# A fused attention and MLP kernel: the first batch's token softmax and state reads are placed later in the written order, and two pairs of loads change places

## The chip, the cores and the metric

The kernel runs on one core of one Trainium2 chip. The metric is the device time of a run in microseconds (us); before is the median of 3 runs. Besides the runs there is one profiled execution, whose span and time are given below.

## What is computed

```
x (8, 8, 512, 64), state (8, 8, 32, 64), float32          # batch, head, rows, 64 columns
scores  = x @ state^T / 8;   a  = softmax(scores)          # 512 x 32 per head
xread   = a @ state                                        # 512 x 64
scores2 = state @ x^T / 8;   a2 = softmax(scores2)         # 32 x 512 per head
sread   = a2 @ x                                           # 32 x 64
X = [xread; sread], heads side by side -> (8 * 544, 512)
h = X @ w_in (512 x 2048);  g = max(h, 0) + alpha * min(h, 0)
out = g @ w_out (2048 x 512), float32                      # (4352, 512)
```

For the 512 token rows of a batch the kernel never forms xread: it multiplies the states into w_in first (`m` = state @ w_in, per batch 256 x 2048) and then the softmax weights by `m`. The 32 state rows of each batch (sread) are collected and go through w_in and w_out together as a ninth "batch".

## The kernel before

Everything is done in the order of a string, `ORDER` (lines 17 to 102), which is read token by token at the end of the function. A token is a step with its arguments; each engine gets its instructions in that order and waits by semaphores. Nothing is reordered. `a`, `v` and `p` in a token name the engine that does a copy or a shift: ScalarE (ACT), VectorE (DVE), GpSimd (POOL). In `F.0.8.4` batch 0, slice 8 of 16, PSUM bank 4 are meant.

The steps, b being the batch:

- Loads, all issued by POOL's queue: `lx0` (x of batch 0 in two halves, L178), `lst` (states, L191), `wi.f` (w_in, four blocks of 512 columns, L197), `wo.i` (w_out, four blocks of 512 rows, L203), `lx.b` (x, L162).
- x transposed: for batches 0 and 1 on PE (`xt`, L277, copied out by `xo`, L282); for the others by a DMA transpose from SP's queue (`xd`, L269) into a rotating buffer `xT`.
- `Z` (L216): matmuls of zeros that fill PE at the start. `stt`, `str` transpose the states; `sto`, `sro` copy them out.
- `sc.b` (L291): both score products in one, into the PSUM tile `two` (two banks). `sc.0.0` and `sc.0.1` are batch 0's halves; `sc.0` computes them again as a whole.
- State softmax (over 32 states, for the token rows): `sb` transpose (L324, L326), `smax` (L332), `ssh` shift (L338), `sexp` (L344), `ssum` (L348, L349), `snorm` (L352), `wb` transpose back (L360) into `aT`, the weights. Batch 0 goes through it in halves.
- Token softmax (over 512 tokens, for the state rows): `tm` maximum (L372, L375), `te.b.g` exponential (L383) from `two`, `tsum` reciprocal (L393), `tn` norm on POOL (L397), `tt` DMA transpose from SP's queue (L401), `rd` the reads a2 @ x on PE (L416), `rdo` copy out (L427). Its buffers `e2` have two places, and a place is free when `tt` has landed.
- `m.b.f` (L441): 8 matmuls in 64 x 32 tiles, in `two` or in two single banks; `mo` copies them to `m`, one bank at a time (L463).
- First product: `F` (L474, two matmuls), or `f` for one half of it (L495). `N` on ACT (L506) and `G` on DVE (L514) make g of it and set the bank free.
- Second product: `S.b.q.j` (L526, two matmuls; eight of them make a 128 x 512 output), `O` copies it out (L564) and SP's queue writes it (L567). `R`, `L`, `RO`, `LO` do the same for the state rows and the last output in pieces.

There are six single banks and `two`. Each new use of a bank waits for the copy or the `G` that empties it. `xg` (x as loaded) has 4 places in SBUF, `xT` 2, `m` 7.

Of the kernel before, what the change touches and what calls it, by code (L numbers as in the profile page):

```python
# [46 lines left out]
S.1.3.5 N.2.8 S.1.3.6 G.2.7 F.2.6.2 O.1.0.a N.2.6 m.3.3.1.0 G.2.8 sc.4 rd.1.5 snorm.p.3 F.2.5.3
G.2.6 mo.3.3.a.0 F.2.14.1 rdo.1.a wb.3 N.2.5 tsum.3 S.2.1.0.2 F.2.11.5 mo.3.3.a.1 G.2.5 S.1.3.7
N.2.14 F.2.10.0 F.3.4.3 G.2.14 N.2.11 S.2.1.1 F.3.1.1 lx.5 O.1.3.v N.3.4 S.2.1.2 N.2.10 G.2.11 tt.2
S.2.0.0.4 S.2.1.3 S.2.0.1 G.2.10 F.3.14.5 F.3.9.0 S.2.1.4 tn.3.1 N.3.1 N.3.9 G.3.1 S.2.1.5 S.2.0.2  # L50
G.3.4 tn.3.0 N.3.14 tm.4 F.3.3.1 F.3.8.3 G.3.14 N.3.8 G.3.9 S.2.1.6 S.2.1.7 S.2.0.3 S.2.3.0.5 N.3.3
xd.5 O.2.1.a tt.3 sb.4 G.3.8 smax.4 F.3.6.0 F.3.2.2 te.4.0 S.2.3.1 S.2.3.2 N.3.6 N.3.2 F.3.13.3
S.2.0.4 te.4.1 ssh.p.4 N.3.13 G.3.3 G.3.6 S.2.0.5 F.3.7.1 G.3.2 S.2.0.6 N.3.7 S.2.0.7 sexp.4 G.3.13
G.3.7 S.2.3.3 S.2.3.4 S.2.3.5 m.6.0 O.2.0.v m.5.1.0.2 mo.6.0.a.1 mo.5.1.a.1 rd.3.3 mo.6.0.v.0
rdo.3.a mo.5.1.v.0 rd.2.1 m.4.1.4.2 ssum.4 sc.5 m.4.3.0.3 rdo.2.a S.2.3.6 mo.4.1.a.1 mo.4.1.a.0 tm.5
tsum.4 snorm.p.4 F.3.5.1 mo.4.3.a.0 mo.4.3.a.1 F.3.0.2 F.3.10.4 N.3.0 S.2.3.7 O.2.3.a S.2.2.0.0
S.2.2.1 F.3.11.3 G.3.0 wb.4 S.2.2.2 S.3.3.0.5 F.3.15.2 S.3.3.1 N.3.5 lx.6 G.3.5 te.5.0 te.5.1 N.3.10
N.3.15 S.2.2.3 F.3.12.1 S.2.2.4 N.3.11 S.3.3.2 lx.7 N.3.12 G.3.10 G.3.15 F.4.6.4 N.4.6 tn.4.0
# [577 lines left out]
```

## Time and profile before

| | us |
|---|---|
| median of 3 runs (218.6 to 219.0) | 218.71 |
| profiled execution, its own time | 219.66 |
| its span | 217.9 |
| PE busy | 210.6 |
| first `f` on PE (L495) | 16.23 |
| first `S` on PE (L526) | 20.89 |
| ACT copies of the states (L259), two | 9.56 to 11.64 |

The span is the time from the first to the last instruction on the chip; what lies around it (1.76 us) is not seen in the trace. A line of the timeline has the start, the length, the engine, the line of the kernel, the operation, what it writes and reads, how many, and in brackets the idle time before it and who ended it. Matmuls overlap, so a pair that starts every 0.43 us is shown as 0.59 us long. PEld is PE's weight load. A line of the windows has, for each stretch, the busy time of PE, PEld, DVE, ACT and POOL with the number of instructions, then the granted PE clock, the busy share of the DMA engines and what they moved. DMA issues take time on the queue's engine; the time to landing is counted from the issue.

Time to landing of the first loads, from the views of their tiles: w_in block 0, issued at 4.05, took 7.6 us; x of batch 1, issued at 4.80, 9.5; w_in 1 at 5.68, 11.6; w_out 0 at 12.45, 7.3; w_in 2 at 15.75, 7.2; w_out 1 at 16.55, 8.5; w_in 3 at 17.29, 10.3; w_out 2 at 23.53, 7.4; x of batch 2 at 25.90, 7.7; w_out 3 at 29.98, 8.9; x of batch 3 at 41.34, 9.0. The DMA transposes of x took 7.7 (issued at 33.71), 5.3 (50.48), 3.7, 3.7, 4.8 and 3.7 us; those of the token weights 3.5, 6.9 (47.21), 3.9, 3.1, 3.3, 3.1 and 4.2.

### The profile page before, as it was taken

The page shows a single profiled execution, that of the slowest core. Times are in us where ns is not written, and L with a number is a line of the kernel's source. Part 1 is how long each engine was busy: PE and PEld are TensorE (multiplying, and loading weights), DVE is VectorE, ACT ScalarE, POOL GpSimd, SP SyncE. Part 2 cuts the span into 40 slices and gives each one's busy share as a digit, 9 for nine tenths or more (in the row PEclk, how much of TensorE's full clock was granted, in tenths as well). Part 3 has the DMA queues.
Part 4 walks back from the last instruction along what each step waited for, and adds up shares of the span by engine and source line. Part 5 has one row for each costly group of instructions (what it writes and reads, how often), then busy time and mean ns, then how long its engine had stood idle before and what let it go on. Part 6 is the DMA issues. An engine that isn't in the chain of part 4 may idle for free.

```text
span 217.9 us, 4311 instructions
## 1 busy us (share of the span) xinstructions
PE 210.6 (97%) x1698; PEld 104.2 (48%) x1698; DVE 165.2 (76%) x250; ACT 137.4 (63%) x271; POOL 71.0 (33%) x58
## 2 busy tenths in 40 slices
...
GB/s 69 188 199 206 200 171 117 206 196 113 92 143 100 92 245 101 51 88 187 249 55 99 96 48 53 0 99 48 50 148 3 46 48 51 48 33 15 51 96 144
DMA packets 41748, 23.12 MB, mean 106 GB/s; under 512 B 24192, under 2 KB 38016, under 8 KB 41728
## 3 DMA queue, kind: packets, MB, share of 16 engines
q0 software_dynamic: 12704, 8.62, 28.5%
...
q14 instruction: 7, 0.06, 0.1%
...
## 4 chain that ended last, share of the span: by engine, by line
PE 84%; DMA 9%; DVE 3%; POOL 1%; issue 1%; ACT 0%; POOLq 0%
PE o L526 47%; PE h L474 23%; DMA xT<-xg 4%; DMA w_in_sb<-in_moe_w_in_dram 3%; PE m_ps L441 3%; PE h L483 3%; PE o L574 3%; DMA xg<-in_x_dram 2%; PE o L546 2%; PE sr_ps L416 2%; PE sc L291 1%; POOL an L352 1%; DVE ts L326 1%; DVE m L463 1%; DVE mx L332 1%
## 5 line engine op out<-in xcount | busy, mean ns | idle before, releaser
L526 PE MATMUL o<-w_out_sb,gt 128*128 128x512 f16 x496 | 125.3, 379 | 0.9 <-DMA w_out_sb<-in_moe_w_out_dram 0.9
L506 ACT ACTIVATE neg<-h 128x512 f32<-128x512 f32 (+1 forms) x144 | 77.1, 579 | 47.8 <-PE h L474 38.4
L514 DVE SCALAR_TENSOR_TENSOR gt<-neg,oma_sb,h 128x512 f16<-128x512 f32 x128 | 89.9, 738 | 16.5 <-ACT neg L506 15.6
L526 PEld LDWEIGHTS <-gt 128*128 128x128 f16 x496 | 47.3, 98 | 56.4 <-issue 4.5
L474 PE MATMUL h<-aT,m 128*128 128x512 f16 x250 | 68.3, 379 | 0.0
L474 PEld LDWEIGHTS <-m 128*128 128x128 f16 x250 | 24.1, 98 | 28.4 <-issue 0.6
L397 POOL TENSOR_SCALAR e<-e,r 128x512 f16<-128x512 f16 x16 | 25.0, 1566 | 20.4 <-DVE r L393 16.6
L463 ACT CAST m<-m_ps 128x512 f16<-128x512 f32 x50 | 27.1, 606 | 4.6 <-PE m_ps L441 4.3
L352 POOL TENSOR_TENSOR an<-ts,r 128x1024 f16<-128x1024 f32 (+1 forms) x9 | 15.4, 1719 | 33.2 <-DVE r L349 14.8
L338 POOL TENSOR_TENSOR ts<-ts,mx 128x1024 f32<-128x1024 f32 (+1 forms) x9 | 15.5, 1720 | 30.9 <-DVE mx L332 30.9
L564 ACT COPY osb<-o 128x512 f32<-128x512 f32 x22 | 12.9, 591 | 14.9 <-PE o L526 14.9
L441 PE MATMUL m_ps<-w_in_sb,stT 64*32 64x512 f16 x256 | 11.3, 383 | 0.6 <-DMA w_in_sb<-in_moe_w_in_dram 0.4
L383 ACT ACTIVATE e<-sc,nb 128x512 f16<-128x512 f32 x16 | 11.1, 700 | 1.1 <-DVE nb L375 1.1
L360 DVE STREAM_TRANSPOSE aT<-an 128x1024 f16<-128x1024 f16 (+1 forms) x9 | 10.1, 1120 | 1.9 <-POOL an L352 1.9
L514 DVE SCALAR_TENSOR_TENSOR gs<-neg,oma_sb,h 128x256 f16<-128x256 f32 x16 | 7.5, 476 | 4.5 <-ACT neg L506 4.5
L463 DVE CAST m<-m_ps 128x512 f16<-128x512 f32 x14 | 9.1, 679 | 2.0 <-ACT m L463 1.6
L372 DVE TENSOR_REDUCE nb<-sc 128x2 f32<-128x1024 f32 x8 | 9.6, 1202 | 0.5 <-PE sc L291 0.5
L332 DVE TENSOR_REDUCE mx<-ts 128x32 f32<-128x1024 f32 (+1 forms) x9 | 9.8, 1091 | 0.0
L348 DVE TENSOR_REDUCE r<-ts 128x32 f32<-128x1024 f32 (+1 forms) x9 | 9.8, 1087 | 0.0
L483 PE MATMUL h<-XS,w_in_sb 128*128 128x256 f16 x64 | 9.4, 273 | 0.0
L584 DVE COPY osr<-o 128x512 f32<-128x512 f32 x1 | 0.7, 692 | 11.3 <-PE o L574 11.3
L344 ACT ACTIVATE ts<-ts 128x1024 f32<-128x1024 f32 (+1 forms) x9 | 8.6, 960 | 0.2 <-POOL ts L338 0.2
...
## 6 DMA issues: line engine op xcount, KB each, us to landing
...
```

The costliest lines, as they stand in the source:

```text
L332: nc.vector.tensor_reduce(cols(live["mx", b], j, S // N), blocks(cols(live["ts", b], j, S)), AX.X, ALU.max)
L338: engine(e).tensor_tensor(ts, ts, over_blocks(cols(live["mx", b], j, S // N)), ALU.subtract)
L352: engine(e).tensor_tensor(blocks(cols(live["an", b], j, S)), blocks(cols(live["ts", b], j, S)), over_blocks(cols(live["r1", b], j, S // N) ...
L397: nc.gpsimd.tensor_scalar_mul(e2, e2, live["r2", b][:, g : g + 1])
L441: nc.tensor.matmul(t[N * k : N * (k + 1), :], st_head(b, h)[64 * r : 64 * r + 64, :], w_in_sb[64 * r : 64 * r + 64, c, 512 * f : 512 * (f ...
L463: copier(e)(m_tile(b)[:, f, g, :], live["mp", b, f][g])
L474: nc.tensor.matmul(h.rearrange("p (r j s) -> p r j s", r=2, j=2), ms[b][:, f, g, 128 * j : 128 * (j + 1)], weights(b, g), start=(g == 0), ...
L483: nc.tensor.matmul(h, w_in_sb[:, c, 128 * jc : 128 * (jc + 1)], XS[:, c].rearrange("p q n b -> p (q n b)"), start=(c == 0), stop=(c == n_c ...
L506: nc.scalar.activation(neg, h, RELU, bias=0.0, scale=-1.0)
L514: nc.vector.scalar_tensor_tensor(gt, negs.pop((b, jc)), oma_sb[:, jc : jc + 1], h, ALU.mult, ALU.add)
L526: nc.tensor.matmul(outs[b, q], gts[b, jc][:, 128 * q : 128 * (q + 1)], w_out_sb[:, jc, :], start=(jc == 0), stop=(jc == n_jc - 1),)
L564: copier(e)(osb, t)
```

## The change

- Batch 0's whole scores (`sc.0`), its token softmax (`tm.0`, `te.0`, `tsum.0`, `tn.0`, `tt.0`) and its state reads (`rd.0`, `rdo.0`) leave the first phase. They now stand among batch 1's and 2's work: `sc.0` between `sc.2` and `sc.3`, `rd.0` beside `rd.1`. Its x, transposed and not, is held until then.
- Hence the buffers: `xg` has 5 places, `xT` 3, `m` 6.
- The loads on POOL's queue: w_in 1 ahead of x1, w_in 2 ahead of batch 0's shift, w_out 2 and 3 right behind w_in 3, and so the last w_out ahead of x2; x4 ahead of x3.
- Batch 1's x is transposed on PE after the first `f` instead of before it. Ten `m` stand ahead of the first `S` instead of seven, and the zero matmuls are split otherwise (82 before, 91 after).
- The second half of batch 0's shift goes from POOL to DVE (`ssh.v.0.1`); several copies go from one of DVE and ACT to the other.
- The order of the middle is written anew; from `O.6.0` on (batches 6 and 7) it is the same but for the numbers of the banks.

The order up to batch 4, and the buffers:

```diff
@@ ORDER @@
-stc lx0.0 lx0.1 oma id Z.1.20 stt.0 Z.2.18 xt.0.0.0.1 sto.a xt.0.1.0.2 xo.0.0.0.v lst xo.0.1.0.v
-Z.0.6 sc.0.0 xt.0.1.1.3 xt.0.0.1.4 sb.0.0 xo.0.0.1.v smax.0.0 xo.0.1.1.a str.0.5 sc.0.1 str.1.0 wi.0
-sro.0.a lx.1 wi.1 ssh.p.0.0 sb.0.1 Z.1.3 sc.0 Z.5.7 m.0.0.1.2 sro.1.a sexp.0.0 smax.0.1 m.3.0.3.4
-ssh.p.0.1 tm.0 mo.0.0.a.1 sexp.0.1 ssum.0.0 m.1.0.5.0 ssum.0.1 te.0.1 te.0.0 mo.1.0.v.1 wo.0
-mo.1.0.a.0 snorm.p.0.0 mo.3.0.a.1 Z.2.28 xt.1.1.1.2 xt.1.1.0.5 mo.0.0.a.0 snorm.p.0.1 wb.0.0
-mo.3.0.a.0 m.2.0 xt.1.0.1.0 xo.1.1.0.v xt.1.0.0.4 f.0.0.0.1 f.0.1.0.5 wi.2 mo.2.0.a.0 wb.0.1
-mo.2.0.a.1 f.0.1.1 xo.1.0.0.v N.0.1 m.0.1.3.4 f.0.0.1 mo.0.1.a.1 m.1.1 xo.1.1.1.v N.0.0 xo.1.0.1.v
-mo.0.1.v.0 f.0.2.0.2 F.0.3.0 f.0.2.1 F.0.4.3 mo.1.1.v.0 mo.1.1.a.1 F.0.7.4 G.0.1 N.0.2 G.0.0 wo.1
-F.0.5.5 N.0.3 G.0.2 wi.3 m.4.0 N.0.4 S.0.0.0.1 N.0.5 G.0.3 tsum.0 S.0.1.0.2 N.0.7 mo.4.0.a.1 G.0.4
-S.0.0.1 S.0.1.1 G.0.5 mo.4.0.a.0 tn.0.1 m.0.2.0.3 sc.1 G.0.7 S.0.2.0.5 mo.0.2.a.0 tm.1 m.1.2.0.4
-wo.2 tn.0.0 mo.0.2.a.1 mo.1.2.a.0 S.0.2.1 lx.2 sb.1 F.0.6.3 F.0.9.0 mo.1.2.a.1 N.0.6 S.0.2.2 S.0.0.2
-N.0.9 G.0.6 S.0.1.2 smax.1 te.1.1 te.1.0 F.0.11.4 G.0.9 ssh.p.1 F.0.8.3 wo.3 N.0.8 N.0.11 S.0.0.3
-S.0.1.3 m.0.3 G.0.8 F.0.10.0 mo.0.3.a.0 N.0.10 sexp.1 S.0.2.3 mo.0.3.v.1 xd.2 G.0.11 G.0.10
-S.0.3.0.3 m.1.3 S.0.3.1 mo.1.3.a.0 F.0.14.4 S.0.2.4 F.0.13.0 N.0.14 tt.0 ssum.1 S.0.0.4 S.0.1.4
-S.0.0.5 S.0.3.2 G.0.14 F.0.12.4 N.0.13 G.0.13 F.0.15.0 snorm.p.1 N.0.12 N.0.15 mo.1.3.a.1 wb.1
-S.0.3.3 S.0.1.5 S.0.3.4 G.0.12 S.0.2.5 G.0.15 S.0.3.5 F.1.2.4 S.0.2.6 N.1.2 F.1.0.0 tsum.1 S.0.2.7
-N.1.0 S.0.1.6 S.0.1.7 G.1.2 O.0.2.a sc.2 m.2.1.4.5 S.0.0.6 O.0.1.a F.1.7.2 mo.2.1.a.0 mo.2.1.a.1
-G.1.0 F.1.1.0 tm.2 sb.2 F.1.3.4 N.1.7 S.0.0.7 S.0.3.6 N.1.1 G.1.1 N.1.3 tn.1.0 O.0.0.a te.2.0
-F.1.5.5 S.0.3.7 N.1.5 G.1.3 F.1.9.0 S.1.1.0.1 G.1.7 F.1.4.4 smax.2 O.0.3.a S.1.1.1 tn.1.1 G.1.5
-rd.0.2 te.2.1 N.1.9 G.1.9 m.2.3 F.1.6.3 N.1.4 rdo.0.a F.1.12.5 N.1.6 lx.3 G.1.4 F.1.13.2 N.1.12
-F.1.8.0 G.1.6 G.1.12 S.1.2.0.4 N.1.13 G.1.13 ssh.p.2 N.1.8 S.1.1.2 F.1.11.3 G.1.8 F.1.10.5 N.1.11
-S.1.2.1 N.1.10 G.1.11 G.1.10 S.1.2.2 sexp.2 S.1.1.3 ssum.2 F.1.14.2 F.1.15.0 snorm.p.2 mo.2.3.a.0
-S.1.1.4 mo.2.3.a.1 S.1.1.5 m.3.2 m.4.2.3.5 N.1.14 tt.1 tsum.2 N.1.15 G.1.14 mo.3.2.a.1 S.1.1.6
-S.1.2.3 S.1.2.4 mo.3.2.a.0 mo.4.2.a.0 G.1.15 mo.4.2.a.1 S.1.2.5 S.1.1.7 xd.3 O.1.1.a m.3.1.2.0
-m.2.2.3.5 sc.3 wb.2 tn.2.1 S.1.2.6 S.1.2.7 mo.3.1.a.1 F.2.15.1 S.1.0.0.0 mo.2.2.a.0 mo.3.1.a.0
-O.1.2.a lx.4 mo.2.2.a.1 sb.3 N.2.15 S.1.0.1 tm.3 F.2.13.3 N.2.13 G.2.15 S.1.0.2 F.2.4.2 tn.2.0
...
+lx0.0 stc lx0.1 id lst Z.1.20 stt.0 sto.v Z.2.18 xt.0.0.0.1 oma xt.0.1.0.2 xo.0.1.0.v wi.0
+xo.0.0.0.a wi.1 Z.0.6 sc.0.0 xt.0.0.1.3 xt.0.1.1.4 sb.0.0 lx.1 str.1.5 xo.0.0.1.a sro.1.a xo.0.1.1.v
+sc.0.1 str.0.0 smax.0.0 sro.0.a sb.0.1 Z.3.16 m.0.0.1.2 smax.0.1 ssh.v.0.1 wi.2 ssh.p.0.0 sexp.0.0
+mo.0.0.a.0 ssum.0.0 m.2.0.3.4 sexp.0.1 wo.0 mo.0.0.v.1 ssum.0.1 mo.2.0.a.0 m.4.0.5.0 mo.4.0.a.1
+mo.4.0.a.0 m.1.0 Z.1.15 m.3.0.1.3 m.0.1.2.0 snorm.p.0.0 mo.3.0.a.0 mo.2.0.a.1 wb.0.0 snorm.p.0.1
+Z.5.9 f.0.1.0.5 mo.1.0.a.0 mo.3.0.v.1 wb.0.1 wo.1 mo.0.1.v.1 m.2.1.1.4 mo.1.0.a.1 Z.3.7 m.1.1
+f.0.1.1 mo.2.1.v.1 xt.1.0.0.3 mo.0.1.a.0 xo.1.0.0.v xt.1.0.1.2 F.0.4.0 f.0.0.0.4 xo.1.0.1.v f.0.0.1
+F.0.5.3 mo.2.1.a.0 xt.1.1.0.1 N.0.1 mo.1.1.a.0 wi.3 N.0.4 F.0.3.2 N.0.0 G.0.1 G.0.4 N.0.5 N.0.3
+xt.1.1.1.5 f.0.2.0.0 xo.1.1.0.v xo.1.1.1.a F.0.7.1 G.0.0 G.0.5 mo.1.1.a.1 f.0.2.1 N.0.2 m.1.2.4.5
+wo.2 mo.1.2.a.1 G.0.3 F.0.6.3 wo.3 sc.1 m.0.2.2.5 G.0.2 sb.1 N.0.7 tm.1 mo.0.2.a.1 G.0.7 S.0.3.0.0
+mo.0.2.a.0 S.0.3.1 N.0.6 G.0.6 S.0.2.0.5 S.0.2.1 S.0.1.0.2 smax.1 S.0.1.1 mo.1.2.a.0 te.1.1 lx.2
+F.0.8.4 S.0.3.2 N.0.8 F.0.9.1 S.0.2.2 F.0.10.3 S.0.1.2 N.0.9 G.0.9 S.0.1.3 G.0.8 te.1.0 N.0.10 m.0.3
+mo.0.3.v.1 F.0.11.1 S.0.3.3 S.0.2.3 ssh.p.1 G.0.10 mo.0.3.a.0 m.1.3 N.0.11 F.0.13.4 sexp.1 N.0.13
+G.0.11 F.0.14.3 F.0.12.1 ssum.1 S.0.2.4 snorm.p.1 S.0.3.4 S.0.2.5 N.0.14 S.0.3.5 G.0.14 N.0.12
+G.0.12 G.0.13 F.0.15.3 S.0.1.4 S.0.1.5 xd.2 wb.1 S.0.2.6 N.0.15 S.0.3.6 tsum.1 mo.1.3.a.0 S.0.1.6
+mo.1.3.a.1 F.1.11.1 G.0.15 F.1.13.4 N.1.11 N.1.13 G.1.11 S.0.1.7 F.1.7.3 S.0.2.7 O.0.1.a S.0.3.7
+G.1.13 F.1.9.1 N.1.7 G.1.7 F.1.2.2 O.0.2.a tn.1.1 N.1.9 F.1.3.4 N.1.2 F.1.0.5 N.1.0 S.0.0.0.3 tn.1.0
+N.1.3 G.1.9 G.1.2 G.1.0 S.0.0.1 S.0.0.2 m.3.1.1.2 O.0.3.a sc.2 F.1.4.5 F.1.1.0 mo.3.1.a.0 G.1.3
+N.1.1 S.0.0.3 tm.2 sb.2 mo.3.1.a.1 S.0.0.4 F.1.12.4 N.1.4 N.1.12 S.0.0.5 G.1.1 S.0.0.6 S.0.0.7
+te.2.0 F.1.5.1 lx.4 S.1.0.0.2 G.1.4 F.1.15.0 te.2.1 F.1.6.5 smax.2 N.1.5 m.2.3 O.0.0.a N.1.6
+mo.2.3.a.0 S.1.0.1 mo.2.3.a.1 G.1.5 G.1.12 S.1.2.0.3 lx.3 F.1.8.1 N.1.15 S.1.2.1 N.1.8 G.1.6
+S.1.1.0.4 S.1.1.1 tt.1 ssh.p.2 G.1.15 S.1.1.2 S.1.2.2 sc.0 m.5.1.5.0 sexp.2 G.1.8 F.1.10.1 ssum.2
+S.1.1.3 S.1.2.3 snorm.p.2 mo.5.1.a.1 N.1.10 F.1.14.0 S.1.2.4 tm.0 mo.5.1.a.0 S.1.1.4 G.1.10 S.1.0.2
+S.1.0.3 N.1.14 G.1.14 S.1.1.5 xd.3 te.0.1 te.0.0 S.1.2.5 sc.3 m.2.2.5.1 S.1.1.6 S.1.1.7 mo.2.2.a.0
+wb.2 O.1.1.a F.2.2.0 mo.2.2.a.1 sb.3 tsum.0 F.2.5.5 N.2.2 S.1.0.4 N.2.5 smax.3 F.2.6.4 N.2.6 G.2.2
+S.1.2.6 S.1.0.5 F.2.4.1 S.1.0.6 S.1.2.7 tn.0.1 N.2.4 O.1.2.a G.2.5 G.2.6 ssh.p.3 G.2.4 F.2.13.0
+S.1.0.7 N.2.13 S.1.3.0.5 F.2.0.4 O.1.0.a F.2.3.1 S.1.3.1 N.2.0 N.2.3 sexp.3 F.2.12.3 N.2.12 tm.3
+S.1.3.2 tn.0.0 G.2.13 F.2.14.2 F.2.15.0 N.2.14 tt.0 S.1.3.3 G.2.0 N.2.15 F.2.1.4 G.2.3 ssum.3 N.2.1
+F.2.11.1 te.3.1 te.3.0 G.2.14 S.1.3.4 S.1.3.5 S.1.3.6 G.2.15 F.2.9.2 G.2.1 F.2.7.0 tsum.2 snorm.p.3
+N.2.9 tn.2.0 S.1.3.7 xd.4 G.2.12 N.2.7 m.3.3 rd.0.4 G.2.9 rd.1.3 F.2.10.2 rdo.0.v O.1.3.a S.2.0.0.5
+mo.3.3.a.1 S.2.0.1 tsum.3 lx.5 G.2.7 N.2.11 G.2.11 rdo.1.a tn.3.1 mo.3.3.a.0 N.2.10 wb.3 m.3.2.4.3
+sc.4 m.5.0.0.1 mo.3.2.a.0 S.2.0.2 mo.5.0.v.1 S.2.0.3 G.2.10 mo.3.2.a.1 S.2.1.0.4 mo.5.0.a.0 F.2.8.3
+N.2.8 S.2.1.1 tn.3.0 F.3.13.1 F.3.1.0 N.3.13 S.2.1.2 N.3.1 sb.4 F.3.4.2 G.2.8 F.3.14.3 G.3.13 tm.4
+G.3.1 S.2.1.3 tn.2.1 N.3.14 F.3.9.1 S.2.1.4 S.2.0.4 N.3.9 smax.4 S.2.0.5 G.3.14 tt.2 S.2.0.6 S.2.0.7
+N.3.4 G.3.4 F.3.3.0 G.3.9 te.4.1 S.2.1.5 te.4.0 S.2.1.6 ssh.p.4 O.2.0.a N.3.3 S.2.2.0.3 m.4.3.2.5
+m.6.0 tsum.4 xd.5 sexp.4 tn.4.0 mo.6.0.a.1 tt.3 S.2.1.7 S.2.2.1 mo.4.3.v.0 mo.6.0.a.0 G.3.3
+S.2.3.0.1 ssum.4 F.3.11.2 mo.4.3.a.1 S.2.3.1 F.3.8.0 N.3.11 G.3.11 S.2.3.2 S.2.3.3 snorm.p.4 O.2.1.a
+F.3.2.5 N.3.8 S.2.2.2 F.3.6.4 N.3.2 G.3.8 S.2.3.4 N.3.6 F.3.15.2 F.3.7.0 S.2.3.5 S.2.3.6 S.2.3.7
+N.3.15 S.2.2.3 N.3.7 m.4.2 G.3.2 G.3.6 wb.4 G.3.15 O.2.3.a m.4.1.5.4 rd.2.1 rd.3.2 mo.4.2.v.0
+mo.4.2.a.1 G.3.7 mo.4.1.a.1 sc.5 m.5.3.4.0 rdo.2.a rdo.3.v tm.5 mo.4.1.a.0 mo.5.3.a.0 S.2.2.4
...
@@ -158,7 +158,7 @@
     def load_x(b):
-        xg = xgs[b] = att.tile([128, H, 2, 2, D], F16, name=f"xg_{b}", tag="xg", bufs=4)
+        xg = xgs[b] = att.tile([128, H, 2, 2, D], F16, name=f"xg_{b}", tag="xg", bufs=5)
@@ -172,7 +172,7 @@
-    xgs[0] = att.tile([128, H, 2, 2, D], F16, name="xg_0", tag="xg", bufs=4)
+    xgs[0] = att.tile([128, H, 2, 2, D], F16, name="xg_0", tag="xg", bufs=5)
     def load_x0(g):
@@ -262,7 +262,7 @@
     def x_tile(b):
-            live["xT", b] = att.tile([128, H, 2, 128], F16, name=f"xT_{b}", tag="xT", bufs=2)
+            live["xT", b] = att.tile([128, H, 2, 128], F16, name=f"xT_{b}", tag="xT", bufs=3)
     def x_transposed_dma(b):
@@ -431,7 +431,7 @@
     def m_tile(b):
-            ms[b] = moe.tile([128, n_f, 2, 512], F16, name=f"m_{b}", tag="m", bufs=7)
+            ms[b] = moe.tile([128, n_f, 2, 512], F16, name=f"m_{b}", tag="m", bufs=6)
     def m_matmuls(t, b, f, g):
```

More of the change, by code (lines that the diff above doesn't have):

```diff
@@ L47 @@
[L47 to L58, printed above, removed]
@@ new lines @@
+F.3.0.1 F.4.6.2 mo.5.3.a.1 sb.5 N.4.6 N.3.0 lx.6 F.3.5.5 S.2.2.5 xd.6 F.3.12.4 S.2.2.6 S.2.2.7 G.3.0
+F.3.10.0 N.3.12 N.3.5 G.4.6 O.2.2.a F.4.8.1 G.3.5 S.3.3.0.2 N.4.8 te.5.0 S.3.3.1 G.3.12 F.4.5.3
+S.3.3.2 N.4.5 smax.5 S.3.3.3 S.3.1.0.5 N.3.10 ssh.p.5 G.4.8 G.4.5 te.5.1 F.4.11.4 G.3.10 N.4.11
+S.3.3.4 S.3.1.1 F.4.7.1 N.4.7 F.4.3.3 F.4.4.0 sexp.5 S.3.1.2 S.3.3.5 G.4.7 S.3.1.3 F.4.1.1 ssum.5
+N.4.3 N.4.1 S.3.1.4 S.3.3.6 S.3.1.5 S.3.1.6 tsum.5 G.4.11 S.3.1.7 S.3.0.0.4 S.3.3.7 G.4.3 O.3.1.a
+m.6.1.3.5 sc.6 G.4.1 F.4.13.1 sb.6 S.3.0.1 N.4.4 G.4.4 S.3.0.2 mo.6.1.a.1 snorm.p.5 S.3.2.0.5
@@ new lines @@
+S.3.0.3 mo.6.1.a.0 F.4.2.3 O.3.3.a F.4.0.2 N.4.0 S.3.0.4 tn.4.1 S.3.2.1 F.4.14.0 S.3.2.2 S.3.0.5
+N.4.2 wb.5 tm.6 S.3.2.3 G.4.2 S.3.0.6 N.4.13 S.3.2.4 G.4.13 tn.5.0 G.4.0 S.3.2.5 smax.6 S.3.0.7
+N.4.14 F.4.9.3 S.3.2.6 N.4.9 tt.4 te.6.1 F.5.3.1 O.3.0.v F.4.10.2 tn.5.1 lx.7 te.6.0 G.4.14 N.5.3
+G.4.9 F.5.0.4 N.4.10 F.5.13.0 S.3.2.7 S.4.1.0.3 S.4.1.1 G.5.3 ssh.p.6 O.3.2.a tsum.6 S.4.1.2
+F.4.12.1 N.5.0 S.4.1.3 S.4.1.4 N.5.13 xd.7 G.4.10 F.4.15.5 tt.5 G.5.0 S.4.0.0.2 N.4.12 S.4.0.1
+tn.6.1 G.5.13 m.5.2.4.0 m.6.3 S.4.1.5 G.4.12 tn.6.0 N.4.15 mo.5.2.v.1 G.4.15 mo.6.3.v.0 mo.5.2.a.0
```

78 lines of the change are left out of this document (32 added, 46 removed).

## The prediction

> **What bounds the kernel now.** First the page: TensorE (PE) is busy all through, at full clock.
>
> ```profile
> PE 210.6 (97%) x1698; PEld 104.2 (48%) x1698; DVE 165.2 (76%) x250; ACT 137.4 (63%) x271; POOL 71.0 (33%) x58
> ...
> PE 84%; DMA 9%; DVE 3%; POOL 1%; issue 1%; ACT 0%; POOLq 0%
> ```
>
> The chain of waits is PE for 84%, so time is won only by less PE work after PE fills up, or fewer waits on it. The timeline by steps shows where it fills: the first product matmul (`f`) starts at 16.23, the first of the second product (`S`) at 20.89. From there the work is regular, and the holes are countable.
>
> ```profile
> 20.89 1.90 PE L526 MATMUL o<-w_out_sb,gt 128*128 128x512 f16 x8
> ...
> 38.97 0.59 PE L526 MATMUL o<-w_out_sb,gt 128*128 128x512 f16 x2 [0.85 <-DMA w_out_sb<-in_moe_w_out_dram]
> ...
> 41.41 0.14 PEld L291 LDWEIGHTS <-stT 64*32 64x32 f16 x16 [0.61 <-DMA xT<-xg]
> ```
>
> The second line is PE out of work until the last w_out block, the third until batch 2's transposed x. Next the POOL queue, which issues the loads:
>
> ```profile
> 23.53 0.81 POOL L203 DMA_DIRECT2D w_out_sb<-in_moe_w_out_dram  x1
> ...
> 25.90 0.94 POOL L162 DMA_DIRECT2D xg<-in_x_dram  x1
> ...
> 29.98 0.79 POOL L203 DMA_DIRECT2D w_out_sb<-in_moe_w_out_dram  x1
> ```
>
> The last w_out load goes out behind x of batch 2, the token norms and a state shift. Last, the windows: early on VectorE (DVE) and ScalarE (ACT) are as full as PE.
>
> ```profile
> 20.00:24.00 4.00, 3.83 (x45) 1.36 (x43) 4.00 (x8) 3.76 (x9) 2.00 (x2) 1.00 1.24 205
> 24.00:28.00 4.00, 4.00 (x26) 1.79 (x26) 3.97 (x6) 3.88 (x9) 2.80 (x3) 1.00 1.23 193
> 28.00:32.00 4.00, 3.97 (x32) 1.50 (x30) 3.47 (x7) 3.60 (x6) 2.65 (x2) 1.00 1.31 176
> ```
>
> (PE, PEld, DVE, ACT, POOL, clock, DMA, GB/s.)
>
> **A unit for PE work.** Start to start, a pair of 512-column matmuls takes 0.432 us (L526 x8, say: 1.73 in the chain), `m` 0.22, `sc` 0.23, `rd` 0.55; a switch into these tiled forms and back adds 0.23 (`S`, `m`, `F` take 0.53, 0.34, 0.44). After 20.89 before has 248 S, 121 F of batches 0 to 7, 25 m, 7 sc, 8 rd, 15 tiled groups and an end piece (F of batch 8, R, L) that both kernels share: 191.9 us. PE's last matmul ends at 214.7, so the waits are 214.7 - 20.9 - 191.9 = 1.9. They are found: 1.02 at 37.5 (last w_out), 0.31 in the group at 88, 0.24 at 22.2 (w_in block 2), 0.18 at 41, and 0.2 in crumbs.
>
> **The change, part by part.**
>
> *PE work.* Before computes batch 0's scores twice too (`sc.0.0`, `sc.0.1`, then `sc.0`), so the recomputation is moved, not added. The four transposes of x1 (0.23 each) go behind the first `f`, but stand before the first `S`, as do 10 m against 7, sc.1 and 8 F or f triples against 7. So after its first `S` the changed kernel has one F (0.43) and three m (0.66) less; sc, rd and the number of groups (15) are equal: 191.9 - 1.1 = 190.8 us.
>
> *When the first S starts.* It needs `G.0.2`, last of a DVE row. Batch 0's scores still wait for the states' landing (8.94) and two 1 us copies on ACT end at 11.64 as before, so the state exponential of half 0 ends near 12.2; taking 1.4 us of `tm` off DVE and 1.8 of `te` off ACT gives nothing here, since seven copies of m come into their place. The second half's shift goes to DVE, which has no such row: between 0.65 (a 512-wide reduction, L332) and 1.05 (POOL's, L338), I take 0.65 as the nearest DVE row; it ends at 12.1, or 12.5, which costs at most 0.3. Sum and reciprocal of half 0 end at 13.1. From there DVE goes without a pause: copy 0.63, sum 0.9, transpose 0.7, copy 0.65, transpose 0.7, two copies 1.3, two copies of xT 0.8, two G 1.35, xT 0.4, four G 2.65 (nine G took 6.05) = 10.1, to 23.2. ACT is ahead of it: from 12.64 one exponential 0.53, nine copies at 0.49 and the N and copies between end `N.0.2` at 22.3. x1 must be there at 17.3. Loads land in order, at 11.7, 14.3, 17.3, 19.8, 23.0, 25.1, 27.6, 30.9, 33.6 (issue plus time to landing, block by block; DMA moves about 200 GB/s throughout); with w_in 1 ahead of x1 and w_in 2 ahead of w_out 0, x1 lands at 17.3 and w_out 0 at 23.0. So the first S starts at 23.3; not before 23.0 (w_out 0), and by 24.2 if each of some 15 handovers costs 0.06 more.
>
> *Queues.* w_in 2 now passes POOL's shift, w_out 2 and 3 and x2 pass batch 0's token norms (2 x 1.57). Up to seven loads stand in the queue where before had five; if POOL were held until it drained, its next work is batch 1's shift, which waits for DVE (23.2 + 1.24 + 1.48 + two G 1.35 + 1.2 = 28.5), nine us later, so I cost it at nothing. The last w_out takes x2's old place, 33.6, and is needed at 35.5 (12.2 us of PE work behind the first S): the 1.02 is gone. x2 lands at 36.5 and its transpose is next on SP; it took 7.7 beside the last w_out, 3.7 to 5.3 elsewhere, so it is there by 41.8, needed at 42.6 (19.0 us and a switch behind the first S). [...]
>
> *The moved chain.* For batch 0 between 52 and 72 us come one sc, two DVE instructions (1.21, 0.27), two exponentials and their reads (1.8 on ACT), a reciprocal (0.15), two POOL norms (3.1), a DMA transpose on SP (1.3 of issue, 3.1 to 3.9 to landing), 32 rd matmuls and a copy (0.45). From the first S on DVE has by these rows 15.0 us of work to batch 2's scores where PE has 19.0 (17.1 against 18.9 before), so throughput covers it; if that cover went, it would cost DVE's 1.6. What is new are waits. `xd.3` (x3's transpose) reuses xT of batch 0, which `sc.0` reads, so SP issues it at 52.7 and `sc.3` wants it at 57.1 (28.8 and 33.8 us of PE work behind the first S): 4.4 us for what takes 3.7 to 5.3. Behind `xd.3` on SP stand batch 1's outputs, whose buffers have four places. `te.0` waits on ACT for the landing of `tt.1` (issued near 49.5; 3.1 to 6.9), with `te.0`'s own end at 57.0 against 57.1. `te.3` waits for `tt.0` (65.1 + 3.5 against 68.7), and behind it stand N of batch 2. `te.4` waits for `tt.2` (rd.0 ends at 71.9, then POOL's x5 issue 0.95 and three norms 4.7, so 77.6 + 3.5 against 81.1). x4 is loaded ahead of x3, which then lands at 51.5 at the latest (9.0 us beside the outputs, plus one block), in time. I take 0.15 for `sc.3`, 0.1 each for `te.3` and `te.4`, 0.3 for crumbs as before's (0.2, plus part of a group's 0.31): 0.65. Bounds: 0 below, as no wait can give; 1.5 above (0.9 at `sc.3` and 0.3 at each of the two).
>
> *Sum.* 23.3 + 190.8 + 0.65 = 214.75 against 214.7: +0.05. The profiled execution took 219.66, 217.9 of span and 1.76 around it; the median of the runs is 218.71. The difference goes onto the median: 218.8.
>
> **Rivals.**
>
> 1. *The moved chain binds (slower).* Place: `sc.3`. From a landing of `xd.3` over 4.4 us on, PE waits for the excess; with the 5.3 of the same transpose in before (issued at 50.48), 0.9 instead of 0.15: 219.5. For it: that very row, and `tt.1` may still be in flight; against: the four later ones, 3.7 to 4.8.
> 2. *The start is late (slower).* DVE's row from 13.1 to 23.2 has no slack, and at 24.2 the sum is +0.95: 219.7. For it: in the windows above both helpers are full; against: nine G did run at 0.67 each.
> 3. *No new wait (faster).* First S at 23.0, waits 0.1: 213.9, -0.8: 217.9. For it: before loses only 0.4 after 41.6 with like chains; against: every one of three waits must come out well.
> 4. *PE falls back to its first pace (slower).* In the timeline four x transposes take 0.40 start to start at 6.6 us and 0.23 at 8.3, twenty zero matmuls 2.31 at the start and 28 later 1.72: PE is slower by 0.57 until about 8 us, though the granted clock reads 1.00. In the changed kernel PE has little between 13.7 and 17 but zero matmuls, three m and two f. If it then fell back for as long as the thinnest stretch of before lasted (6 to 10 us, 3.27 of 4 busy), 4 us of stream would give 2.3: 1.7 late, 220.5. Against: after just that stretch the pace was full. [...]
>
> **How the numbers follow.** Forecast 0.38 (own range 218.3 to 219.2), rival 1 0.20, rival 2 0.17, rival 3 0.22, rival 4 0.03. 0.2% is 0.44 us, about what a measurement of this kernel can tell from no change. Of the forecast 0.33 lies within it, 0.03 below, 0.02 above: faster 0.25, same 0.33, slower 0.42. The range takes in all but the far sides of rivals 3 and 2 and rival 4: 217.8 to 220.2.
>
> **What would show it.** The first S near 23.3 with `G.0.2` just before; no wait on w_out at 35.5; `sc.2` without a wait; `xd.3` issued right behind `sc.0`; a wait at `sc.3` under 0.3. A first S before 22.9, or a wait over 1 us at any of the three `te` or at `sc.3`, makes it wrong.

## The result, and the profile after

The kernel before took 218.86 us (median of 6 runs beside the changed kernel, 218.46 to 219.32), the changed kernel 219.70 us (219.50 to 219.81, 6 runs): a ratio of 1.0034, 95% interval 1.0017 to 1.0050. That is slower by 0.34%, or 0.84 us. The profiled execution of the changed kernel took 219.71, span 217.9.

Its page: PE's busy time, its chain, and the second product, which no longer waits for a load of w_out (before: 0.9).

```profile
PE 210.6 (97%) x1707; PEld 103.5 (47%) x1707; DVE 163.7 (75%) x247; ACT 139.6 (64%) x275; POOL 69.8 (32%) x57
...
PE 82%; DVE 7%; DMA 5%; POOL 2%; ACT 1%; issue 1%; POOLq 0%
...
L526 PE MATMUL o<-w_out_sb,gt 128*128 128x512 f16 x496 | 124.5, 379 | 0.0
```

The chain is PE for 82% (84 before) and now DVE for 7% (3 before). The timeline of PE at the start (start, duration, engine, line, what; in brackets the idle time and what ended it):

```profile
14.68 0.41 PE L441 MATMUL m_ps<-w_in_sb,stT 64*32 64x512 f16 x8 [0.80 <-DMA w_in_sb<-in_moe_w_in_dram]
15.02 0.68 PE L216 MATMUL z<-zero 128*128 128x128 f16 x9
15.75 0.38 PE L495 MATMUL h<-aT,m 128*128 128x512 f16 x1
...
16.40 0.56 PE L216 MATMUL z<-zero 128*128 128x128 f16 x7
...
17.46 0.61 PE L277 MATMUL xT_ps<-ident,xg 128*128 128x128 f16 x8
...
23.04 1.25 PE L526 MATMUL o<-w_out_sb,gt 128*128 128x512 f16 x5
```

The first product starts at 15.75 (before 16.23) and the first S at 23.04 (before 20.89). Between 14.68 and 17.46, until x1 has landed at 17.3, PE has three groups of `m`, two halves of a first product and zero matmuls. The last matmul ends at 214.78 (its start plus its unit).

To compare the two kernels the kernel before was profiled a second time (first experiment below); that execution took 218.71, the median itself, while the one the prediction was made from took 219.66. Against it:

| us | before, second execution | after | difference |
|---|---|---|---|
| first S | 20.67 | 23.04 | +2.37 |
| PE work behind it (units of the prediction) | 191.9 | 190.8 | -1.1 |
| the rest up to the last matmul: waits | 1.20 | 0.94 | -0.26 |
| last matmul ends | 213.77 | 214.78 | +1.01 |
| span | 216.94 | 217.93 | +0.99 |

So the waits did become fewer, and the loss is that the first S comes 2.37 later while only 1.1 of work has been moved ahead of it. Where that happens is seen by crediting each matmul with its unit (zero matmuls with nothing) and adding up what PE has done by a given time; the total is 197.75 in both kernels:

| useful PE work done by | 14 | 17 | 20 | 23 | 26 | 38 | 60 | 100 us |
|---|---|---|---|---|---|---|---|---|
| before, second execution | 3.72 | 5.47 | 8.05 | 10.45 | 13.10 | 24.28 | 45.12 | 83.97 |
| after | 3.93 | 4.69 | 7.55 | 9.59 | 12.54 | 23.51 | 44.53 | 82.97 |
| after less before | +0.21 | -0.78 | -0.50 | -0.86 | -0.56 | -0.77 | -0.59 | -1.00 |

By 17 us the changed kernel is 0.78 behind, and at the later times of the table it is 0.5 to 1.0 behind; in between it swings by some tenths, as the two kernels do their groups of `m` at different times. The windows view of the zero matmuls alone (line 216) shows the same three microseconds; columns are window, length, PE busy, weight loads, clock, DMA, GB/s. Before, second execution:

```profile
14.00:17.00 3.00, 0.26 (x5) 0.08 (x2) 1.00 1.24 205
```

and after:

```profile
14.00:17.00 3.00, 1.24 (x16) 0.90 (x16) 1.00 1.38 202
```

Zero matmuls fill 1.24 of the three microseconds instead of 0.26. In the kernel before, x1 landed at 14.9 in this execution and its four transposes (0.88) were done then, beside `m.2.0` and three halves of `f`; in the changed kernel w_in 1 goes ahead of x1, which lands at 17.3.

The chain of waits says what the changed kernel is held by after that (start, length, what):

```profile
4.79 9.85 DMA w_in_sb<-in_moe_w_in_dram
...
15.09 0.62 PE z L216 x9
...
16.47 0.50 PE z L216 x7
...
18.64 1.38 DVE gt L514 x2
...
20.36 2.63 DVE gt L514 x4
22.98 1.16 DVE ts L324
...
33.77 1.93 POOL an L352
...
35.72 1.25 DVE aT L360
...
37.02 1.04 PE h L474 x4
```

and before, in its second execution:

```profile
4.87 10.05 DMA xg<-in_x_dram
...
14.97 0.62 PE xT_ps L277 x8
...
32.72 1.56 PE o L526 x8
34.28 6.13 DMA xT<-xg
```

Before runs from x1's landing through PE alone to 34 (in its first execution the chain reached PE at 22.96 by the load of w_in 2 instead). The changed kernel runs from w_in 1's landing through PE, two groups of zero matmuls among it, to x1's transposes, then over VectorE and POOL, through batch 0's G and batch 1's softmax, to the first product of batch 1 at 37.02. PE has four waits between 30 and 37 (0.10, 0.07, 0.21, 0.19); the first, for a copy of `m.0.3`, stands in the kernel before as well.

### The profile page after: what moved, and what is told of

It is laid out like the page before. It is cut to its first block, busy times and chain, and to the rows that moved or that the text cites. A ratio compares the mean times of both kernels' runs of the same rounds, so it can differ in the third digit from the quotient of the medians.

```text
span 217.9 us, 4323 instructions
## 1 busy us (share of the span) xinstructions
PE 210.6 (97%) x1707; PEld 103.5 (47%) x1707; DVE 163.7 (75%) x247; ACT 139.6 (64%) x275; POOL 69.8 (32%) x57
## 4 chain that ended last, share of the span: by engine, by line
PE 82%; DVE 7%; DMA 5%; POOL 2%; ACT 1%; issue 1%; POOLq 0%
PE o L526 45%; PE h L474 23%; DMA w_in_sb<-in_moe_w_in_dram 5%; PE h L483 3%; PE o L574 3%; PE m_ps L441 3%; DVE gt L514 3%; PE o L546 2%; PE sr_ps L416 2%; POOL an L352 1%; PE sc L291 1%; DVE m L463 1%; DVE aT L360 1%; DVE r L348 1%; POOL xg L178 1%
## 5 line engine op out<-in xcount | busy, mean ns | idle before, releaser
L506 ACT ACTIVATE neg<-h 128x512 f32<-128x512 f32 (+1 forms) x144 | 77.9, 581 | 42.0 <-PE h L474 32.7
L463 ACT CAST m<-m_ps 128x512 f16<-128x512 f32 x50 | 27.8, 609 | 7.6 <-PE m_ps L441 5.5
L397 POOL TENSOR_SCALAR e<-e,r 128x512 f16<-128x512 f16 x16 | 24.9, 1560 | 17.7 <-issue 10.5
L564 ACT COPY osb<-o 128x512 f32<-128x512 f32 x26 | 15.5, 597 | 17.3 <-PE o L526 17.3
L338 POOL TENSOR_TENSOR ts<-ts,mx 128x1024 f32<-128x1024 f32 (+1 forms) x8 | 14.4, 1801 | 35.7 <-DVE mx L332 35.7
L441 PE MATMUL m_ps<-w_in_sb,stT 64*32 64x512 f16 x256 | 11.8, 382 | 1.6 <-DMA w_in_sb<-in_moe_w_in_dram 1.5
L324 DVE STREAM_TRANSPOSE ts<-sc 128x1024 f32<-128x1024 f32 x7 | 8.7, 1237 | 1.0 <-PE sc L291 1.0
```

Of the source, the lines that this page charges most:

```text
L338: engine(e).tensor_tensor(ts, ts, over_blocks(cols(live["mx", b], j, S // N)), ALU.subtract)
L397: nc.gpsimd.tensor_scalar_mul(e2, e2, live["r2", b][:, g : g + 1])
L441: nc.tensor.matmul(t[N * k : N * (k + 1), :], st_head(b, h)[64 * r : 64 * r + 64, :], w_in_sb[64 * r : 64 * r + 64, c, 512 * f : 512 * (f ...
L463: copier(e)(m_tile(b)[:, f, g, :], live["mp", b, f][g])
L506: nc.scalar.activation(neg, h, RELU, bias=0.0, scale=-1.0)
L564: copier(e)(osb, t)
```

## The experiments

The question is where the 0.84 us come from: from the rearranged start, from the moved chain, or from the baseline. Kernels sent together ran on one chip beside runs of the kernel before; every ratio is to those. Tokens are those of `ORDER`; `-` and `+` lines show what is moved.

**Before and after once more.** No edit. The question was where the profiled execution of before had its extra 0.95 us.

> The kernel before, unchanged, profiled once more. Its profiled execution took 219.66 us where the median of its runs is 218.86; the changed kernel's took 219.71 with a median of 219.70. Both spans were 217.9. Theory A (the usual run of before has a shorter wait for the last w_out block or for batch 2's transposed x): a usual run's trace has the first f at about 16.2 again, but waits at 37.5 and 41 of about 0.4 instead of 1.2, and a span near 217.1. Theory B (the usual run starts sooner: x of batch 0 landed at 6.57 in the profiled run of before and at 5.61 in that of the changed kernel, from the same instructions): x lands at 5.6, the first f is at 15.4 to 15.9, the waits at 37.5 and 41 stay near 1.2, span near 217.1. Theory C (the profile alone makes before longer): own time 219.6 again beside runs of 218.8.

> The changed kernel, unchanged, on the same chip as the others. Theories A and B: 219.7 again, 0.3 to 0.4% above before. If the difference was one of the chips used: within 0.2% of before. The first S near 23.0, waits of about 0.9 behind it, wherever x lands between 5.6 and 6.6, since the states' landing and ACT's copies come between.

Before: 218.83 us, ratio 1.0005 [0.9986, 1.0025], profiled at 218.71. After: 219.78, ratio 1.0033 [1.0013, 1.0054]. In the second execution of before (timeline of PE) the last w_out block is waited for much less:

```profile
37.31 0.59 PE L474 MATMUL h<-aT,m 128*128 128x512 f16 x2
38.02 0.59 PE L526 MATMUL o<-w_out_sb,gt 128*128 128x512 f16 x2
38.45 0.59 PE L474 MATMUL h<-aT,m 128*128 128x512 f16 x2
```

Two matmuls of `F` at 37.31 fill 0.43, so 0.28 is left until 38.02, where the execution shown before the prediction had 1.02. PE had to wait for the block's landing at 37.98. The first S is 0.22 earlier (20.67). These two, 0.74 and 0.22, are the difference of the spans (217.88 and 216.94). So it is above all the wait for the last w_out that differs between these two executions, which is theory A. Of the 35 runs of before beside this one, 5 took 219.66 or more. The other waits behind the first S agree to 0.05. The changed kernel repeats: its waits agree to 0.01 us, though x of batch 0 was transposed 0.8 later in the second execution (6.41 against 5.61).

**The order of the last w_out and x2.**

```diff
 e3 (before): - S.0.2.1 lx.2 sb.1 ... ssh.p.1 F.0.8.3 wo.3 N.0.8
              + S.0.2.1 wo.3 lx.2 sb.1 ... ssh.p.1 F.0.8.3 N.0.8
 e4 (after):  - F.0.6.3 wo.3 sc.1 ... te.1.1 lx.2
              + F.0.6.3 sc.1 ... te.1.1 lx.2 wo.3
```

> Before with one thing of the change: the last w_out load goes out ahead of x of batch 2 instead of behind it. If the wait for the last w_out is a real loss of before and x2 has room: the 1.0 at 37.5 goes and 217.9 to 218.2 us. If x2's transpose then comes too late: x2 lands near 36.5, sc.2 waits about 0.6 to 1.0 more, and the time stays within 0.2% of before. If most runs of before lose little at that place (theory A): no gain, or a loss of up to 0.5.

> The changed kernel with the last w_out load behind x of batch 2, as before has it, issued back to back with it at about 19 us. If the order of these two alone decides: w_out 3 lands at 36 to 37 (beside x2's transpose perhaps 38), S.0.2.6 wants it at 35.5, so PE waits 1 to 2.5 us and the time is 220.5 to 222. If the transpose is then so much earlier that nothing is lost: 219.7.

The first took 219.08, ratio 1.0009 [0.9987, 1.0032]; the second 219.84, ratio 1.0045 [1.0029, 1.0061]. In the first the wait for w_out is gone, and PE waits for x2's transpose in its place:

```profile
41.95 0.41 PE L291 MATMUL sc<-xT,stT 64*32 64x256 f16 x16 [1.46 <-DMA xT<-xg]
```

This execution took 220.23, 1.15 above the median of its runs, so the usual wait is likely shorter. In it, changing the two loads about gives one wait for the other. In the changed kernel the order is free: with x2 first, the last w_out landed at 35.6, just when it was wanted, and no wait came. The loss that was expected there did not come. So what the change wins from its loads goes with issuing both early (17 to 19 us, where before has 25 to 30), not with turning these two.

**The token chain taken away in both places.** Left out are `sc.0`, `tm.0`, `te.0`, `tsum.0`, `tn.0`, `tt.0` and `rd.0`:

```diff
 - sc.0 tm.0 te.0.1 te.0.0 tsum.0 tn.0.1 tn.0.0 tt.0 rd.0 rdo.0
 + rdc.0   (ahead of rdo.1: batch 1's reads copied a second time, into batch 0's place)
```

> The kernel before without batch 0's token softmax and state reads in the first phase: sc.0, tm.0, te.0, tsum.0, tn.0, tt.0 and rd.0 are left out, and the place of batch 0's reads is filled with a second copy of batch 1's. Left out of PE's work after the first S: rd.0, 0.53 us. Theory A (what the change loses it loses in the first phase, where x1's transposes and three more m stand ahead of the first S; the token chain itself costs little more than its PE work in either place): the chain takes 1.55 us of DVE, 1.8 of ACT and 3.1 of POOL out of the start, but x1's landing near 15 still holds the start, so the first S comes at 20.0 to 20.6 against 20.67, the waits for the last w_out and for sc.2 (0.28 and 0.18) go because POOL issues the loads 3 us sooner; time 217.3 to 217.9. Theory B (the chain in the first phase was a real burden, which the change takes away and then pays for at its new place): the first S comes at 19.5 or sooner and the time is 216.8 or less.

> The changed kernel without the same chain: sc.0, tm.0, te.0, tsum.0, tn.0, tt.0 and rd.0 left out at their new places, batch 0's reads filled with a second copy of batch 1's. Left out of PE's work: sc.0 and rd.0, 0.75 us. Theory A: the first S stays at 23.0 to 23.2 and the time is 219.75 less 0.75, so 218.9 to 219.1: still not faster than the kernel before, though it does less. Theory B (the moved chain brings waits to PE beyond its own matmuls): some 0.4 to 0.8 more goes, 218.3 to 218.6, and waits behind the first S fall from 0.95 to about 0.4.

Before without the chain: 218.36, ratio 0.9964 [0.9943, 0.9985], 0.72 less than the runs beside it (219.08). Its start was later (first `m` at 12.01, first S at 21.04), so it is counted from the first f: to the last matmul it takes 196.69 against 197.44 in the second execution of before, so 0.75 less, 0.53 of it the reads. This is less than theory A expected and far from theory B: by these two traces the chain in the first phase held PE up by about 0.2 us. After without it: 220.46, slower than with it, which neither theory had. The reason is in the edit: the second copy was put on VectorE and the first on ScalarE (timeline of ScalarE):

```profile
73.85 0.44 ACT L429 CAST XS<-sr_ps 128x128 f16<-128x128 f32 x1 [1.16 <-DVE XS L426]
```

The two copies read one PSUM tile, and ScalarE's began when VectorE's had ended; `m.3.2` waited for the bank that it empties and `sc.4` for the copy of `m.3.3` behind it on ScalarE, 1.31 in all. Without that wait the last matmul would end at 213.97, 0.81 before the changed kernel's, with 0.75 of matmuls left out. Against the second execution of the changed kernel (214.89) it would be 0.92. So the moved chain costs its matmuls and 0.1 to 0.2 us of waits; but this subtracts a wait from a trace, and the kernel without it was not run.

**The deferral alone, with the start as before.**

```diff
 - sc.0 tm.0 te.0 tsum.0 tn.0 tt.0 rd.0 rdo.0          (first phase)
 - S.1.1.5 m.3.2 m.4.2.3.5 ... lx.4
 + S.1.1.5 sc.0  m.4.2.3.5 ... tm.0 te.0.1 te.0.0 tsum.0 lx.4 tn.0.1 tn.0.0 ... tt.0 ... m.3.2 ... rd.1.5 rd.0.s
   xg 5, xT 3, e2 3, m 6 buffers; tt.1 ahead of its old place; rd.0.s shares rd.1's bank
```

> The kernel before with the deferral alone: batch 0's token chain is taken out of the first phase and put at the second batch's, in the place that m.3.2 had; m.3.2 gets a group of its own behind te.3; rd.0 and rd.1 share a PSUM bank; xg 5, xT 3, e2 3 and m 6 buffers; the start is otherwise as before. PE's work after the first S grows by sc.0 (0.23) and a group (0.23). Theory A: first S at 20.0 to 20.6, the waits for the last w_out and for sc.2 gone (0.46), so about 218.2 to 218.8: not slower than before, and 0.9 or more below the changed kernel. Theory B (the chain costs at its new place): waits of 0.5 us or more at sc.3, te.3 or rd.0, 219.3 or more.

220.68, ratio 1.0078 [1.0047, 1.0109]. The first S came at 20.65 where before has 20.67: 1.55 us less on VectorE and 1.8 less on ScalarE in the first phase brought nothing. And at its new place the chain was badly put (timeline of ScalarE, then of PE):

```profile
55.93 0.69 ACT L383 ACTIVATE e<-sc,nb 128x512 f16<-128x512 f32 x1 [1.41 <-DVE nb L375]
```

```profile
56.60 0.39 PE L528 MATMUL o<-w_out_sb,gt 128*128 128x512 f16 x1 [0.66 <-DVE gt L516]
57.92 0.41 PE L291 MATMUL sc<-xT,stT 64*32 64x256 f16 x16 [0.28 <-ACT e L383]
```

`tm.0` stood on VectorE ahead of the G for which PE waited at 56.60, and `sc.3` waited for the late exponential; 0.83 and 0.55 of waits in all, besides 0.32 and 0.54 for w_in 1 and w_in 2. This is theory B's time, but of this placing: in the changed kernel, which has 5.1 us from `sc.0` to `sc.3` where this one has 4.7 with the two waits in it, neither is there.

**The shift on POOL.** `- ssh.v.0.1`, `+ ssh.p.0.1` behind `ssh.p.0.0`.

> The changed kernel with the shift of batch 0's second half on POOL, as in the kernel before, instead of on DVE: 0.69 us less in DVE's row ahead of the first S. Theory A with the DVE row as what sets the first S: first S at 22.4 to 22.6, time 219.1 to 219.3. Rival (the row has slack, or the exponential of the second half then comes late, as POOL needs 1.05 for the shift): first S at 23.0 or later, time 219.7 to 220.3.

219.77, ratio 1.0029 [1.0010, 1.0048]: the same as the changed kernel (219.70 and 219.78). The profiled execution (220.38) started late, with the first `m` at 12.07 and the first S at 23.70; from the one to the other it took 11.63 us, against 11.70 in the changed kernel. So 0.69 us off VectorE's row changes nothing; the chain of waits goes over ScalarE here:

```profile
14.02 4.40 ACT m L463 x9
```

Nine copies of `m` stand in one row there, and then the first N.

**The start undone in the changed kernel.** The bank numbers are changed to match, and 80 zero matmuls are left of 91.

```diff
 - wi.0 wi.1 x1 wi.2 wo.0 ;  m.0.1 f.0.1 m.2.1 Z m.1.1 f.0.1 xt.1 F.0.4 ... m.1.2 F.0.6 sc.1 m.0.2 S.0.3.0
 + wi.0 x1 wi.1 wo.0 wi.2 ;  xt.1 f.0.1 f.0.0 m.0.1 m.2.1 m.1.1 F.0.3 ... S.0.3.0 S.0.2.0 S.0.3.1 S.0.2.1 sc.1 m.0.2 m.1.2
```

> The changed kernel with the order of its start undone, its later part (the deferred token chain, the load order of x4 and x3) kept: loads in the order w_in 0, x1, w_in 1, w_out 0, w_in 2; x1's four transposes ahead of or beside the first f; first S ahead of sc.1, m.0.2 and m.1.2, which share one group. Theory A (the loss is PE work that the change puts behind the first f, when PE is already the bound: 0.88 us of transposes, single groups of m; and w_in 2 ahead of w_out 0, which lands at 22.3): first S at 20.4 to 21.2 instead of 23.1, the last matmul at 213.8 to 214.2, time 218.6 to 219.1, ratio to before 0.998 to 1.001. Rival (VectorE's row of copies and G from 13 us on is the bound, whatever PE's order): PE then waits for G between the first S and 30 us as long as it gained, time 219.5 to 219.9.

220.99, ratio 1.0111 [1.0091, 1.0132]: neither theory's time. The first S came at 20.84 as theory A expected, and by 23 us PE had done 10.29 of useful work, 0.70 more than the changed kernel and 0.16 less than before. Then it lost that and more (timeline of PE):

```profile
23.93 0.41 PE L441 MATMUL m_ps<-w_in_sb,stT 64*32 64x512 f16 x8 [0.26 <-DVE gt L514]
25.28 0.59 PE L526 MATMUL o<-w_out_sb,gt 128*128 128x512 f16 x2 [0.94 <-DMA w_out_sb<-in_moe_w_out_dram]
```

`m.1.2` waited 0.56 for a G that empties its bank, and then no first product was left to do before w_out 1, which landed at 25.2 (in the kernel before 24.7 and 25.1, in the changed one 24.9, and in no trace before 24.6). So PE must have other work until then in each of the orders that were run. Up to 23 us the run shows that the places of x1 and of the steps around it are what holds the changed kernel back; a kernel with the deferral and a start as good as before's was not found. So that the time would be before's with a better start is argued from the sums, not shown by a run. Not tried was the changed kernel without its zero matmuls between 15 and 17. They stand in its chain of waits, but where x1 lands at 17.3 only 0.2 could be won, as its transposes start at 17.46; in two other traces of this start (without the token chain, and with the shift on POOL) x1 landed at 16.67 and 17.05 and its transposes came 0.8 and 1.0 behind it.

**One engine for both copies of `m.4.2`.** The two copies of `m.4.2` in the changed kernel read one PSUM tile (`two`) and go to one tile of `m`, from two engines; before has the same with `m.6.0` (timeline of VectorE there, second execution):

```profile
88.39 1.29 DVE L463 CAST m<-m_ps 128x512 f16<-128x512 f32 x2 [1.16 <-ACT m L463]
```

VectorE's copy began when ScalarE's had ended, 1.16 us idle. The expectations below put this down to the tile that is written. The edit in the changed kernel: `- mo.4.2.v.0 mo.4.2.a.1`, `+ mo.4.2.a.1 mo.4.2.a.0`.

> The changed kernel with both copies of m.4.2 on ScalarE instead of one on VectorE and one on ScalarE. Theory (two engines' copies into one tile go one behind the other, and this makes the waits of 0.23 at sc.5 and 0.27 at m.5.3 near 94 us): these go or fall to 0.1 together, time 219.3 to 219.4. Rival (sc.5 and m.5.3 wait for something else): no change, 219.7 to 219.9.

> The two edits of the changed kernel together (its start undone, the copies of m.4.2 on one engine). If both theories hold and add up: 218.1 to 218.7, ratio 0.996 to 0.999; if VectorE's row bounds the start, 219.1 to 219.5.

The edit alone: 219.43, ratio 1.0031 [1.0014, 1.0047]; with the start undone as well: 220.87, ratio 1.0093 [1.0075, 1.0110], for the reason of the last experiment. In the trace of the first, ScalarE's copies start right behind the matmuls, where before the edit it sat idle for VectorE's (timeline of ScalarE, second execution of the changed kernel, then this run):

```profile
93.75 1.07 ACT L463 CAST m<-m_ps 128x512 f16<-128x512 f32 x2 [0.95 <-DVE m L463]
```

```profile
93.00 1.56 ACT L463 CAST m<-m_ps 128x512 f16<-128x512 f32 x3 [0.22 <-PE m_ps L441]
```

The wait at `sc.5` went from 0.23 to 0.06, that at `m.5.3` from 0.27 to 0.20, and the last matmul ends 0.25 earlier than in the second execution of the changed kernel (214.64 and 214.89). The wait of one engine for the other is seen in the trace; half of the expected gain came, and it is too small to be told apart by the times.

It is not the tile that is written that does it. The copies of `m.5.2` in the changed kernel also go to one tile of `m` from two engines, but out of two single banks, and they run side by side, each started by the matmuls (timelines of ScalarE and of VectorE):

```profile
124.80 0.59 ACT L463 CAST m<-m_ps 128x512 f16<-128x512 f32 x1 [0.61 <-PE m_ps L441]
```

```profile
124.86 0.69 DVE L463 CAST m<-m_ps 128x512 f16<-128x512 f32 x1 [0.89 <-PE m_ps L441]
```

In both kernels every pair of copies by two engines out of `two` runs one behind the other, the second engine idle for the first (in the first executions 0.17 us at `m.1.1`, 0.42 at `m.0.3` and 1.16 at `m.6.0` before, 1.01 at `m.0.3` and 0.94 at `m.4.2` after), and several pairs out of single banks overlap (`m.0.1` before, started at 17.73 and 17.83; `m.5.2` above). So what the pairs that wait have in common is the PSUM tile that both read. `m.4.2` in two single banks was not run.

**Before, with three waits taken away and nothing deferred.**

```diff
 - wi.3 m.4.0 ... tn.0.1 ... wo.2 tn.0.0 ... lx.2 ... wo.3
 + wi.3 wo.2 lx.2 m.4.0 ... tn.0.1 ... tn.0.0 wo.3
 - N.0.7 mo.4.0.a.1 ... mo.4.0.a.0          + mo.4.0.a.1 mo.4.0.a.0 N.0.7
 - mo.6.0.a.1 mo.5.1.a.1 mo.6.0.v.0 mo.5.1.v.0
 + mo.6.0.a.1 mo.5.1.v.1 mo.6.0.a.0 mo.5.1.v.0
```

> The kernel before with three of its waits taken away and nothing deferred: w_out 2 and x2 issued right behind w_in 3, w_out 3 behind batch 0's token norms; both copies of m.4.0 ahead of N.0.7; the copies of m.6.0 both on ScalarE and those of m.5.1 both on VectorE, as one engine's copy into a tile began only when the other's into the same tile had ended (1.16 us of VectorE idle at 88). Theory: 0.28 at the last w_out, 0.18 at sc.2, 0.28 at sc.1 and 0.32 at m.4.3 go, 1.06 in all: 217.7 to 218.1, ratio 0.995 to 0.997, and these gains need no deferral. Rival (the waits return in another place: batch 0's token norms, G.0.7): 218.5 to 219.0.

218.28, ratio 0.9966 [0.9950, 0.9981]: faster than the kernel before, by 0.34%, and so than both. The waits for the last w_out, at `sc.2`, at `sc.1` and at `m.4.3` are gone from the trace, and VectorE's copies at 88.30 no longer wait for ScalarE. A part came back in another place:

```profile
23.55 0.41 PE L441 MATMUL m_ps<-w_in_sb,stT 64*32 64x512 f16 x8 [0.91 <-DMA w_in_sb<-in_moe_w_in_dram]
```

w_in 2, issued at 15.6, landed at 23.5, where in six other traces with this load order up to it, issued at 14.9 to 16.2, it landed at 22.2 to 23.0. Three of the six had w_out 2 and x2 issued right behind it too, so the loads queued behind it do not do this alone; the cause is open. The gain needs no deferral: POOL can issue w_out 2 and x2 ahead of batch 0's token norms.

## Why the prediction was right or wrong

The time, 219.70, lies in the range (217.8 to 220.2) but above the forecast (218.8) and above the likeliest case's own range (218.3 to 219.2). By its bound of 0.2% the change came out slower, the class with the highest chance, while the forecast itself stood at no change.

- **The sum against the profiled execution** held: 0.05 longer was predicted, and the spans are 217.88 and 217.93.
- **What failed is the step "The difference goes onto the median".** The mis-sized term in it is the wait for the last w_out, 1.02, "the 1.02 is gone": in the second execution of before, which took the median time, it is 0.28. The profiled execution was 0.95 above the median of the runs, which the prediction wrote down and did not place; 0.74 of it was this wait, and 0.22 an earlier first S. So the gain was priced by an execution in which it was large. The sum itself gave 214.75 for the last matmul, and 214.78 was measured; laid against the second execution of before, 213.77, it would have said 0.98 longer, and 1.01 was measured.
- **First S** at 23.3, measured 23.04 (23.16 and 23.42 in two others of this start): right in size, and `G.0.2` ended just before it, at 22.98. The row "without a pause" was not: VectorE had one of 0.63 until x1's transposes (17.89), and taking its shift away moved nothing. What VectorE does ahead of x1's transposes was not the bound. x1's landing at 17.3 alone was not either: in the changed kernel without the token chain x1 landed at 16.67, 0.60 sooner, and its transposes (17.49) and the first S (23.07) came no earlier. They stand behind three groups of `m`, two halves of a first product and the zero matmuls in PE's order.
- **PE work and waits.** 23.04 + 190.8 leaves 0.94 of waits behind the first S, where 0.65 were predicted; that this and the first S, 0.26 early, cancel is luck. They were looked for in the moved chain. They were instead in batch 1's softmax (0.10, 0.07, 0.21, 0.19 between 30 and 37) and in the copies out of `two` by two engines near 94 (0.23, 0.27), which add up to 1.07, so the units are good to about 0.1; `sc.3`, `te.3` and `te.4` held nothing up.
- **"`xd.3` (x3's transpose) reuses xT of batch 0"** was wrong. It was issued at 51.81, ahead of `sc.0` at 52.5, so it took another place of xT. It took 5.2 us, and `sc.3` started at 57.57 without a wait, 0.5 behind its landing. Rival 1 has no mechanism here.
- **Queues.** Seven loads outstanding did not hold POOL, as assumed: the issues from 15.1 to 18.1 follow one another. The last w_out landed at 32.5 and x2 at 35.2 (predicted 33.6 and 36.5); `sc.2` had no wait. x2's transpose, with no load beside it, took 3.8 us in both executions, where before, with one beside it, took 7.7 and 6.1. It landed at 39.1, where 41.8 was allowed for. The traces of most kernels go the same way for x2's transpose: 3.8 to 4.0 without a load (the changed kernel, and before with the last w_out first), 5.1 to 7.7 with one (before and four of the edited kernels); but in the changed kernel with its start undone it took 5.8 without one, and x3's in the changed kernel took 5.2 with no load in flight. What lengthens it was not shown.
- **Rival 2** gave 219.7, the measured time, by another way: its first S at 24.2 did not come, and what made the time was the baseline. Rival 3 had the first S right (23.0) and the waits wrong. Rival 4 fell: the two transposes at 17.46 took 0.45 start to start, 0.23 each, as those at 8.3 in the kernel before (0.40 each at 6.6).
